# Forgetting attention into a SiLU MLP on one core: zero matmuls at the start, score tiles and MLP work in a new order, q and k turned together

## The chip, the core and the metric

The kernel runs on one core of a Trainium2 chip. The core has a matrix engine (PE, with its weight loads shown as PEld), a vector engine (DVE), an engine for exp and tanh (ACT), a general engine (POOL, GpSimd), a sync engine (SP) that issues transfers, and 16 DMA engines. The metric is the device time of one execution in microseconds (us).

## What is computed

```python
# q, k, v: (8 batches, 8 heads, 576, 64); f: (8, 8, 576); w_in: (512, 2048); w_out: (2048, 512)
cum = cumsum(log(clip(f, 1e-4, 1)), -1)
scores = q @ k.T / 8 + cum[:, :, :, None] - cum[:, :, None, :]   # causal, else -1e9
x = softmax(scores) @ v                 # heads put side by side: (4608, 512)
h = x @ w_in
out = (h * sigmoid(h)) @ w_out          # (4608, 512) float32
```

## The kernel before

**Tiling.** Two heads make a pair, four pairs a batch, so there are 32 pairs, numbered p = 0 to 31. The sequence of 576 is cut into five blocks, the last of 64 (the tail). Everything is in one hand-written order (`manual_schedule`): each engine runs its instructions in the order in which the code issues them, and waits on what it needs.

**Attention of a pair.** `scores(p, t)` (L270) makes four score tiles, t = 0 to 3, keys by queries: t0 is 512 columns for each head, t1 64 + 448, t2 320 + 192, t3 64. Two PSUM tiles are there for them (`psc`). Each matmul has 64 rows, one head; the two heads go side by side. ACT takes the exp into `uT` (L306). For the first four pairs (`first`, L273) the causal mask is added to the scores ahead of the exp (L300 on DVE, L289 on PE for t2); for all others DVE multiplies `uT` by a 0/1 mask afterwards (L320). `prep_v` (L246, POOL) scales v by the decay into `vaug`. `attend_rows` (L337) does 30 small matmuls `avr` in two groups, LO (12) and HI (18), and DVE divides into `xt` (L358, L359). `turn_pair` (L366) turns `xt` into `xT` with PE and copies on ACT for batches 0 to 3; from batch 4 on (`NTURN`) `turn_batch` (L379) does it by DMA transposes from SP, five or six pieces a batch.

**MLP.** Tokens go in 9 groups of 512. An `m1_chunk` (L391) is four matmuls of 128x512 into `hp`, tanh on ACT (L411) and a product on DVE into `gtile` (L412). An `m2_part` (L419) is four matmuls of an output block `po`; part 0 to 3 use the quarters of `w_out_bf` one after another, and after part 3 ACT copies to `osb` (four buffers) and SP stores it. Each of these units is four matmuls of 128 rows. `hp`, `po`, `avr` and the turns share four PSUM tiles (`big`).

**Order.** `work(n)` (L468) issues n MLP units, each 0.88 on a planner's clock; `spend` advances that clock and runs what `defer` has put off. `pace` (L484) decides how many units a pair gets, with `LAG` as a reserve kept for later batches. The main loop (L646) issues for each pair t0 and t1 together, a third of the units, turns and attention of the pair before, prep of v, loads; t2 and t3 together, a third; attention; and the rest. In batch 1 (pairs 4 to 7) attention's LO and HI parts stand apart.

**Loads.** q and k of batches 0 and 1, and q of batch 2 (`RAW`), come as float32, are cast on POOL (L193, L202) and turned by PE (`turn_first` L206, `transposes` L227; DVE copies them out). The others are loaded and cast by POOL's DMAs in blocks (`load_qk`, L123, tile `mp`), and turned by DMA transposes on SP (`turn_qk`, L131), one for q and one for k, into `qT` and `kT`. From batch 6 on the first blocks' turns are deferred by 9 on the planner's clock. POOL also issues w_in (L548, after the casts of the first three pairs) and w_out (L542, after vaug of pair 4).

**Start.** Batch 0 is done with no MLP work between; the first MLP unit follows its end (L632).

Of the kernel before, what the change touches and what calls it, by code (L numbers as in the profile page):

```python
# [19 lines left out]
def kernel(  # L20
# [19 lines left out]
    NB = 5  # L40
# [9 lines left out]

    const = ctx.enter_context(tc.tile_pool(name="const", bufs=1))
    ident_bf = const.tile([P, P], BF16, name="ident_bf")
    ident_f = const.tile([P, P], FP32, name="ident_f")
# [6 lines left out]
    vaugs = [const.tile([P, NB, 2, DV], BF16, name=f"vaug{i}") for i in range(NVA)]  # L60
    kTs = [const.tile([P, NPB, NB * P], BF16, name=f"kT{i}") for i in range(2)]
    us = [const.tile([P, 2, UW], BF16, name=f"uT{i}") for i in range(3)]

    xp = ctx.enter_context(tc.tile_pool(name="xp", bufs=4))
    qkp = ctx.enter_context(tc.tile_pool(name="qkp", bufs=2))
    vp = ctx.enter_context(tc.tile_pool(name="vp", bufs=2))
# [9 lines left out]
    NTURN = 4  # L76
    LAG = 10.0
    MOST = 9.0
# [5 lines left out]
    def qk_tiles(b):  # L84
        qkT[b] = (qkp.tile([P, NPB, S], BF16, name="qT", tag="qT"), kTs[b % 2])

# [36 lines left out]
    def load_qk(b, c, which):  # L123
        t = sbp.tile([P, DM], BF16, name="mp", tag="mp", bufs=16)
        raw[b, c, which] = t
        nc.gpsimd.dma_start(  # L126
            out=t[: bs[c], :].rearrange("p (h d) -> p h d", h=H),
            in_=(q, k)[which][b, :, c * P : c * P + bs[c], :].rearrange("h p d -> p h d"),
        )

    def turn_qk(b, c, which):  # L131
        if b not in qkT:
            qk_tiles(b)
        n = bs[c]
        nc.sync.dma_start_transpose(
            out=qkT[b][which][:, :, c * P : c * P + n], in_=raw[b, c, which][:n, :]
        )
# [16 lines left out]
    def decay_sum():  # L154
        lnf = f_sb
        cum = evp.tile([BH, S], FP32, name="cum", tag="ev")
        nc.vector.tensor_tensor_scan(
            out=cum[:, :], data0=lnf[:, :], data1=lnf[:, :], initial=0.0,
            op0=ALU.add, op1=ALU.bypass,
        )  # L160
        mid = const.tile([BH, 1], FP32, name="mid")
        nc.vector.tensor_scalar_mul(out=mid[:, :], in0=cum[:, S - 1 : S], scalar1=0.5)
        cumc = cum
        nc.vector.tensor_scalar(
            out=cumc[:, :], in0=cum[:, :], scalar1=mid[:, 0:1], scalar2=None,
            op0=ALU.subtract,
        )
# [38 lines left out]
    def turn_first(which):  # L206
        qk_tiles(0) if 0 not in qkT else None
        m = cast[0, 0, which].rearrange("p c h d -> p c (h d)")
        tp = big([P, SM], BF16, "tpqk")
        for c in range(NB - 1):  # L210
            nc.tensor.transpose(tp[:, c * P : (c + 1) * P], m[:, c, :], ident_bf[:, :])
        nc.vector.tensor_copy(
            out=qkT[0][which][:, 0, 0:SM].rearrange("x (p c) -> x p c", c=NB - 1),
            in_=tp[:, :].rearrange("x (c p) -> x p c", c=NB - 1),
        )

# [53 lines left out]
    def scores(p, t):  # L270
        qT, kT = (x[:, p % NPB, :] for x in qkT[p // NPB])
        u = us[p % 3]
        first = p < NPB  # L273
        sc = psc.tile([P, 2, 512], FP32, name="sc", tag="sc")
# [231 lines left out]
    def retire(p):  # L506
        b, j = divmod(p, NPB)
        if j < NPB - 1:
            return
        for c in range(NB):  # L510
            defer(2.5 + 1.2 * c, lambda c=c: turn_batch(b, c))
        for g in range(b * S // TG, (b + 1) * S // TG):
            c = ((g + 1) * TG - b * S - 1) // P
            defer(6.2 + 1.2 * c, lambda g=g: made(g + 1))
# [8 lines left out]
    for b in range(NEARLY, B):  # L523
        for i, group in enumerate([(0, 1), (2,), (3, 4)]):
            at = NPB * b - 4 + min(i, 1) if b == NEARLY else NPB * b - 7 + i
            late = 1 if b == NEARLY + 1 and len(RAW[NEARLY]) == 2 else 0
            for c in group:
                for w in range(2):
                    if w in RAW.get(b, ()):
                        continue  # L530
                    add(fetch, at + late, load_qk, b, c, w)
                    if b <= NEARLY + 1:
                        to = min(at + late + (2 if b == NEARLY else 3), NPB * b - 2)
                        add(plan, to, turn_qk, b, c, w)
                    elif i == 0 and b - 2 >= NTURN:
                        add(plan, NPB * b - 4, defer, 9.0, partial(turn_qk, b, c, w))
                    else:
                        add(plan, NPB * b - 4 + min(i, 1), turn_qk, b, c, w)
                add(plan, NPB * b - 5 + i + (b == NEARLY), load_v, b, c, nc.sync)
# [11 lines left out]

    with tc.manual_schedule():
        nc.scalar.dma_start(out=f_sb[:, :], in_=f.rearrange("b h s -> (b h) s"))
        load_main(0, 0, 2)
# [17 lines left out]
        make_identity(nc, ident_f)  # L572
        for kT in kTs:
            nc.vector.memset(kT[:, :, S:], 0.0)
        for u in us:
# [17 lines left out]
        load_w(w_in_bf, moe_w_in, DFF // 2, DFF)  # L593
        for w in range(2):
            turn_first(w)
        scores(0, 0)
        turn_first_tails()
        scores(0, 1)
        decay_sum()
        scores(0, 3)  # L600
        transposes(1, 0)
        scores(0, 2)
        decay_turn()
        prep_v(0)
# [8 lines left out]
        for p in range(1, NPB):  # L613
# [32 lines left out]
        for p in range(NPB, NP):  # L646
# [6 lines left out]
            due -= n  # L653
            n1, n2 = (n + 2) // 3, (n + 1) // 3
            n3 = n - n1 - n2
            scores(p, 0)
            scores(p, 1)
            spend(0.4)
            work(n1)
            ahead = RAW.get((p + 1) // NPB, ())  # L660
            rows = NPB < p < NPB * NEARLY
            if 0 in ahead:
                transposes(p + 1, 0)
# [71 lines left out]
```

## Time and profile before

| what | us |
|---|---|
| median of 3 runs (lowest to highest) | 359.81 (359.74 to 360.06) |
| the profiled execution | 359.25 |
| its span | 357.5 |
| PE busy, share of the span | 336.3 (94%) |
| ACT, DVE, POOL busy | 211.9, 191.7, 119.6 |
| moved by DMA | 44.92 MB |

The page gives each engine's busy share in 40 slices of the span, in tenths. Other views are answers of the trace: the timeline of an engine (start, length, engine, source line, operation, output<-inputs, rows*columns and shapes, count; in brackets idle time before it and what ended that), the waits of an engine (total, times, longest), and a source line's own instructions. PE's matmuls overlap and the end of each is modelled, so the cost of a run of matmuls is read from start to start.

### The profile page before, as it was taken

To read this page: it belongs to the slowest core of one execution; us is meant where nothing else is said; L and a number is where in the kernel's file an instruction comes from. 1 tells how busy PE (TensorE), PEld (TensorE's weight loads), DVE (VectorE), ACT (ScalarE), POOL (GpSimd) and SP (SyncE) were. 2 spreads that over 40 slices of the span, in tenths; PEclk is the share of its full clock that TensorE was granted. 3 is DMA by queue.
4 is the path that set the end of the run, shared out by engine and by line. 5 is a ranking of instruction groups with operands and counts; after the bars stand their busy time and mean duration, and the time that the engine had idled before them with its cause. 6 is when DMAs were issued, how large, how long until landed. Compare 5 with 4: busy or idle time off the path is not lost.

```text
span 357.5 us, 7026 instructions
## 1 busy us (share of the span) xinstructions
PE 336.3 (94%) x2656; PEld 168.4 (47%) x2697; DVE 191.7 (54%) x450; ACT 211.9 (59%) x345; POOL 119.6 (33%) x207
## 2 busy tenths in 40 slices
PE   2797989999999999999999999999999999999995
PEld 1455445554555445544454453444444454444442
DVE  4664895538743675348543791567237723744300
ACT  4566674558753986388647764676468615644421
POOL 5563598239554235423564250110301000000000
PEclk9999999999999999999999999999999999999999
DMA  8899999999997998399969994452240014000021
GB/s 220 213 208 315 192 193 222 155 210 170 148 150 117 163 150 78 89 170 142 124 122 152 130 166 123 100 117 75 74 83 31 1 68 118 2 29 29 31 76 71
DMA packets 142514, 44.92 MB, mean 126 GB/s; under 512 B 129616, under 2 KB 136784, under 8 KB 142480
## 3 DMA queue, kind: packets, MB, share of 16 engines
q1 hardware_dynamic: 87664, 33.64, 42.5%
q0 software_dynamic: 54736, 10.69, 38.4%
q8 instruction: 21, 0.34, 0.4%
q10 hardware_dynamic: 80, 0.15, 0.2%
q14 instruction: 13, 0.11, 0.1%
HBM read 36.85 MB, written 9.44 MB: 129 GB/s over the span
## 4 chain that ended last, share of the span: by engine, by line
PE 82%; DVE 6%; ACT 4%; DMA 3%; issue 3%; POOL 1%; SPq 0%; ACTq 0%
PE po L425 33%; PE hp L400 30%; PE avr L349 7%; PE sc L281 7%; DVE gtile L412 2%; ACT uT L306 2%; DMA xT<-xt 2%; PE tpx L371 2%; DVE uT L320 2%; PE tpqk L235 2%; ACT th L411 1%; DMA whole<-in_k_dram 1%; DVE xt L359 1%; PE sc L289 1%; DVE qT L240 1%
## 5 line engine op out<-in xcount | busy, mean ns | idle before, releaser
L400 PE MATMUL hp<-xT,w_in_bf 128*128 128x512 bf16 x556 | 135.8, 380 | 3.2 <-DVE gtile L412 0.8
L425 PE MATMUL po<-w_out_bf,gtile 128*128 128x512 bf16 x555 | 133.7, 379 | 1.4 <-DVE gtile L412 0.4
L412 DVE SCALAR_TENSOR_TENSOR gtile<-th,hp 128x512 bf16<-128x512 bf16 x144 | 96.0, 685 | 52.2 <-ACT th L411 50.3
L306 ACT ACTIVATE uT<-sc 128x1024 bf16<-128x1024 f32 (+1 forms) x128 | 101.3, 850 | 24.9 <-PE sc L281 15.9
L411 ACT ACTIVATE th<-hp 128x512 bf16<-128x512 f32 x144 | 84.8, 613 | 50.0 <-PE hp L400 46.2
L251 POOL TENSOR_TENSOR vaug<-vm,wT 128x512 bf16<-128x512 f32 x64 | 45.4, 729 | 132.7 <-PE avr L349 121.4
L400 PEld LDWEIGHTS <-w_in_bf 128*128 128x128 bf16 x576 | 53.1, 98 | 65.2 <-issue 6.1
L425 PEld LDWEIGHTS <-gtile 128*128 128x128 bf16 x576 | 53.6, 98 | 62.9 <-issue 2.4
L320 DVE TENSOR_TENSOR uT<-uT,mask 128x256 bf16<-128x256 bf16 (+1 forms) x112 | 35.3, 337 | 66.2 <-ACT uT L306 66.0
L434 ACT ACTIVATE osb<-po 128x512 f32<-128x512 f32 x36 | 21.7, 602 | 46.7 <-PE po L425 46.7
L281 PE MATMUL sc<-qT,kT 64*128 64x64 bf16 (+4 forms) x384 | 37.3, 287 | 5.5 <-ACT uT L306 2.2
L349 PEld LDWEIGHTS <-uT 128*128 128x128 bf16 x960 | 33.7, 98 | 6.4 <-issue 0.7
L349 PE MATMUL avr<-vaug,uT 128*128 128x65 bf16 x960 | 36.2, 195 | 0.2 <-POOL vaug L259 0.2
L359 DVE TENSOR_TENSOR xt<-avr,rr 128x384 bf16<-128x384 f32 x64 | 31.4, 491 | 2.3
L281 PEld LDWEIGHTS <-kT 64*128 64x128 bf16 x384 | 15.3, 95 | 30.1 <-issue 21.0
L126 POOL DMA_DIRECT2D mp<-in_k_dram x30 | 25.9, 865 | 1.0 <-DMA mp<-in_k_dram 1.0
L126 POOL DMA_DIRECT2D mp<-in_q_dram x25 | 22.2, 887 | 1.3 <-DMA w_out_bf<-in_moe_w_out_dram 0.5
L358 DVE RECIPROCAL rr<-avr 128x6 f32<-128x6 f32 x64 | 11.7, 183 | 18.6 <-PE avr L349 18.5
L377 ACT COPY xT<-tpx 128x512 bf16<-128x512 bf16 (+7 forms) x32 | 11.2, 404 | 17.0 <-PE tpx L371 16.9
L193 POOL CAST m<-whole 128x512 bf16<-128x512 f32 x20 | 11.9, 607 | 15.0 <-DMA whole<-in_q_dram 12.4
L235 PE MATMUL tpqk<-ident_bf,m 128*128 128x128 bf16 (+1 forms) x90 | 10.9, 241 | 0.3 <-DVE gtile L412 0.3
L235 PEld LDWEIGHTS <-m 128*128 128x128 bf16 (+1 forms) x90 | 7.3, 106 | 6.3 <-issue 1.6
(47 smaller groups left out, 71.8 us busy)
## 6 DMA issues: line engine op xcount, KB each, us to landing
out_dram<-osb SPq DMA_DIRECT2D x36, 256.0 KB, 2.2
vm<-in_v_dram SPq DMA_DIRECT2D x32, 256.0 KB, 4.7
mp<-in_k_dram POOLq DMA_DIRECT2D x24, 128.0 KB, 6.2
whole<-in_q_dram SPq DMA_DIRECT2D x5, 512.0 KB, 9.7
mp<-in_q_dram POOLq DMA_DIRECT2D x20, 128.0 KB, 4.8
w_in_bf<-in_moe_w_in_dram POOLq DMA_DIRECT2D x2, 1024.0 KB, 11.2
w_out_bf<-in_moe_w_out_dram POOLq DMA_DIRECT2D x4, 512.0 KB, 10.7
whole<-in_k_dram SPq DMA_DIRECT2D x3, 512.0 KB, 9.5
```

Source lines behind the costliest of these rows:

```text
L126: nc.gpsimd.dma_start(out=t[: bs[c], :].rearrange("p (h d) -> p h d", h=H), in_=(q, k)[which][b, :, c * P : c * P + bs[c], :].rearrange("h ...
L235: nc.tensor.transpose(tp[:, c * P : c * P + n], m[:n, c, :, :].rearrange("p h d -> p (h d)"), ident_bf[:n, :n],)
L251: nc.gpsimd.tensor_tensor(out=va[:n, c0:c1, :, 0:D], in0=vm[:n, c0:c1, 2 * j : 2 * j + 2, :], in1=wT[:n, c0:c1, 2 * j + b * H : 2 * j + 2 ...
L281: nc.tensor.matmul(sc[:, i, col : col + n], lhsT=kT[r, kb * P : (kb + 1) * P], rhs=qT[r, q0 : q0 + n], start=True, stop=not pe_adds,)
L306: nc.scalar.activation(out=u[:, :, o : o + col], in_=sc[:, :, 0:col], func=ACT.Exp, scale=scale)
L320: nc.vector.tensor_tensor(out=d, in0=d, in1=mk, op=ALU.mult)
L349: nc.tensor.matmul(av[:, qb - lo, i, :], lhsT=u[:, i, o : o + P], rhs=va[:, kb, i, :], start=(kb == 0), stop=(kb == qb),)
L359: nc.vector.tensor_tensor(out=xt[:, lo:hi, 2 * j : 2 * j + 2, :], in0=av[:, :, :, 0:D], in1=r[:, 0:n, :, None].to_broadcast([P, n, 2, D]), ...
L400: nc.tensor.matmul(hp[:, :], lhsT=w_in_bf[:, cc, fc * P : (fc + 1) * P], rhs=xg[g][:, cc, :], start=(cc == 0), stop=(cc == NCC - 1),)
L411: nc.scalar.activation(out=th[:, :], in_=hp[:, :], func=ACT.Tanh, scale=0.5)
L412: nc.vector.scalar_tensor_tensor(out=gte[:, fc, :], in0=th[:, :], scalar=1.0, in1=hp[:, :], op0=ALU.add, op1=ALU.mult,)
L425: nc.tensor.matmul(po[:, :], lhsT=gte[:, fc, tb * P : (tb + 1) * P], rhs=w_out_bf[:, fc, :], start=(fc == 0), stop=(fc == NFC - 1),)
```

## The change

- PE gets matmuls of zeros (`spin`), 34 of 128x512 at the start: seven ahead of the first turn, the others among the turns, score tiles and attention of pairs 0 and 1. Their input `idle` is set to zero first on DVE.
- `turn_first` copies k in two pieces, the first 128 keys ahead.
- Score masks of pairs 4 and 5 are added ahead of the exp (t0, t1, t3).
- q and k share one tile `qkTs` for each parity of the batch. `load_qk` puts both into one tile of twice the width (8 buffers for 16), and one DMA transpose turns both (k alone in batch 2).
- `turn_batch` is issued at once at the end of a batch from 4 on, and the first q/k turns of batches 6 and 7 are no longer deferred.
- `LAG` is 14 for 10.
- In the main loop units are given out by shares of n: in batches 1 and 2 between all four score tiles, from batch 3 on 0.35 after t1, 0.1 and 0.25 after t3, and the rest.

```diff
-    kTs = [const.tile([P, NPB, NB * P], BF16, name=f"kT{i}") for i in range(2)]
+    qkTs = [const.tile([P, 2, NPB, NB * P], BF16, name=f"qkT{i}") for i in range(2)]
...
-    LAG = 10.0
+    LAG = 14.0
...
     def load_qk(b, c, which):
-        t = sbp.tile([P, DM], BF16, name="mp", tag="mp", bufs=16)
-        raw[b, c, which] = t
+        if (b, c) not in raw:
+            raw[b, c] = sbp.tile([P, 2 * DM], BF16, name="mp", tag="mp", bufs=8)
...
-    def turn_qk(b, c, which):
+    def turn_qk(b, c):
...
+        w = [x for x in range(2) if x not in RAW.get(b, ())]
         nc.sync.dma_start_transpose(
-            out=qkT[b][which][:, :, c * P : c * P + n], in_=raw[b, c, which][:n, :]
+            out=qkTs[b % 2][:, w[0] :, :, c * P : c * P + n].rearrange(
+                "x w j n -> x (w j) n"
+            ),
+            in_=raw[b, c][:n, w[0] * DM :],
         )
...
+    def spin(n):
+        ps = big([P, SM], FP32, "spin")
+        for _ in range(n):
+            nc.tensor.matmul(
+                ps[:, :], lhsT=idle[:, 0:P], rhs=idle[:, :], start=True, stop=True
+            )
...
+        for p0, p1 in ((0, P),) if which == 0 else ((0, P // 4), (P // 4, P)):
+            nc.vector.tensor_copy(
...
-        first = p < NPB
+        first = p < NPB + 2 and (t != 2 or p < NPB)
...
         for c in range(NB):
-            defer(2.5 + 1.2 * c, lambda c=c: turn_batch(b, c))
+            turn_batch(b, c)
...
-                    elif i == 0 and b - 2 >= NTURN:
-                        add(plan, NPB * b - 4, defer, 9.0, partial(turn_qk, b, c, w))
-                    else:
-                        add(plan, NPB * b - 4 + min(i, 1), turn_qk, b, c, w)
+                else:
+                    to = NPB * b - 4 + min(i, 1)
+                add(plan, to, turn_qk, b, c)
...
+        nc.vector.memset(idle[:, :], 0.0)
...
-        for w in range(2):
-            turn_first(w)
+        spin(7)
+        turn_first(0)
+        spin(4)
+        turn_first(1)
+        spin(2)
         scores(0, 0)
...
+            def step(share):
+                nonlocal left, part
+                part += share * n
+                k = min(left, int(part + 0.5))
+                part -= k
+                left -= k
+                work(k)
+
             scores(p, 0)
+            spend(0.3)
+            step(0.2 if b <= NEARLY else 0.0)
             scores(p, 1)
-            spend(0.4)
-            work(n1)
+            spend(0.3)
+            step(0.2 if b <= NEARLY else 0.35)
...
-            if early:
-                work(n2 // 2)
+            step(0.1 if b <= NEARLY else 0.0)
             scores(p, 2)
+            spend(0.3)
+            step(0.2 if b <= NEARLY else 0.0)
             scores(p, 3)
-            spend(0.3)
+            spend(0.2)
             if 1 in ahead:
                 transposes(p + 1, 1)
+            step(0.1)
             if rows:
                 attend_rows(p - 1, HI)
-            work(n2 - n2 // 2 if early else n2)
+            step(0.0 if b <= NEARLY else 0.25)
             if b >= NEARLY and j > 0:
                 attend_rows(p - 1)
                 spend(1.2)
-            work(n3)
+            work(left)
```

More of the change, by code (lines that the diff above doesn't have):

```diff
@@ L51 @@
     const = ctx.enter_context(tc.tile_pool(name="const", bufs=1))
+    idle = const.tile([P, SM], BF16, name="idle")
     ident_bf = const.tile([P, P], BF16, name="ident_bf")
@@ L60 @@
     vaugs = [const.tile([P, NB, 2, DV], BF16, name=f"vaug{i}") for i in range(NVA)]
-    kTs = [const.tile([P, NPB, NB * P], BF16, name=f"kT{i}") for i in range(2)]
+    qkTs = [const.tile([P, 2, NPB, NB * P], BF16, name=f"qkT{i}") for i in range(2)]
     us = [const.tile([P, 2, UW], BF16, name=f"uT{i}") for i in range(3)]
     xp = ctx.enter_context(tc.tile_pool(name="xp", bufs=4))
-    qkp = ctx.enter_context(tc.tile_pool(name="qkp", bufs=2))
     vp = ctx.enter_context(tc.tile_pool(name="vp", bufs=2))
@@ L84, in qk_tiles @@
     def qk_tiles(b):
-        qkT[b] = (qkp.tile([P, NPB, S], BF16, name="qT", tag="qT"), kTs[b % 2])
+        qkT[b] = (qkTs[b % 2][:, 0], qkTs[b % 2][:, 1])
     def raw_tile():
@@ L123, in load_qk @@
     def load_qk(b, c, which):
-        t = sbp.tile([P, DM], BF16, name="mp", tag="mp", bufs=16)
-        raw[b, c, which] = t
+        if (b, c) not in raw:
+            raw[b, c] = sbp.tile([P, 2 * DM], BF16, name="mp", tag="mp", bufs=8)
         nc.gpsimd.dma_start(
-            out=t[: bs[c], :].rearrange("p (h d) -> p h d", h=H),
+            out=raw[b, c][: bs[c], which * DM : (which + 1) * DM].rearrange(
+                "p (h d) -> p h d", h=H
+            ),
             in_=(q, k)[which][b, :, c * P : c * P + bs[c], :].rearrange("h p d -> p h d"),
         )
-    def turn_qk(b, c, which):
+    def turn_qk(b, c):
         if b not in qkT:
@@ L134, in turn_qk @@
         n = bs[c]
+        w = [x for x in range(2) if x not in RAW.get(b, ())]
         nc.sync.dma_start_transpose(
-            out=qkT[b][which][:, :, c * P : c * P + n], in_=raw[b, c, which][:n, :]
+            out=qkTs[b % 2][:, w[0] :, :, c * P : c * P + n].rearrange(
+                "x w j n -> x (w j) n"
+            ),
+            in_=raw[b, c][:n, w[0] * DM :],
         )
@@ L211, in turn_first @@
             nc.tensor.transpose(tp[:, c * P : (c + 1) * P], m[:, c, :], ident_bf[:, :])
[L212 to L215, printed above, removed]
+        dst = qkT[0][which][:, 0, 0:SM].rearrange("x (p c) -> x p c", c=NB - 1)
+        for p0, p1 in ((0, P),) if which == 0 else ((0, P // 4), (P // 4, P)):
+            nc.vector.tensor_copy(
+                out=dst[:, p0:p1, :],
+                in_=tp[:, :].rearrange("x (c p) -> x p c", c=NB - 1)[:, p0:p1, :],
+            )
     def turn_first_tails():
@@ L528 @@
                 for w in range(2):
[L529 to L534, printed above, removed]
-                    elif i == 0 and b - 2 >= NTURN:
-                        add(plan, NPB * b - 4, defer, 9.0, partial(turn_qk, b, c, w))
-                    else:
-                        add(plan, NPB * b - 4 + min(i, 1), turn_qk, b, c, w)
+                    if w not in RAW.get(b, ()):
+                        add(fetch, at + late, load_qk, b, c, w)
+                if b <= NEARLY + 1:
+                    to = min(at + late + (2 if b == NEARLY else 3), NPB * b - 2)
+                else:
+                    to = NPB * b - 4 + min(i, 1)
+                add(plan, to, turn_qk, b, c)
                 add(plan, NPB * b - 5 + i + (b == NEARLY), load_v, b, c, nc.sync)
@@ L572 @@
         make_identity(nc, ident_f)
-        for kT in kTs:
-            nc.vector.memset(kT[:, :, S:], 0.0)
+        for t in qkTs:
+            nc.vector.memset(t[:, 1, :, S:], 0.0)
         for u in us:
@@ L593 @@
         load_w(w_in_bf, moe_w_in, DFF // 2, DFF)
-        for w in range(2):
-            turn_first(w)
+        spin(7)
[3 more added lines that the diff above has]
+        spin(2)
         scores(0, 0)
         turn_first_tails()
+        spin(2)
         scores(0, 1)
+        spin(3)
         decay_sum()
         scores(0, 3)
+        spin(1)
         transposes(1, 0)
+        spin(2)
         scores(0, 2)
+        spin(1)
         decay_turn()
@@ L605 @@
         transposes(1, 1)
+        spin(4)
         scores(1, 0)
+        spin(2)
         cast_both(3)
@@ L618 @@
                 transposes(p + 1, 0)
+            if p == 1:
+                spin(2)
             scores(p, 3)
@@ L623 @@
                 turn_pair(p - 2)
+            else:
+                spin(4)
             attend_rows(p - 1, LO)
@@ L653 @@
             due -= n
[L654 to L657, printed above, removed]
-            spend(0.4)
-            work(n1)
             ahead = RAW.get((p + 1) // NPB, ())
             rows = NPB < p < NPB * NEARLY
+            left, part = n, 0.0
+            def step(share):
[5 more added lines that the diff above has]
+                work(k)
+            scores(p, 0)
+            spend(0.3)
+            step(0.2 if b <= NEARLY else 0.0)
+            scores(p, 1)
+            spend(0.3)
+            step(0.2 if b <= NEARLY else 0.35)
             if 0 in ahead:
```

## The prediction

> **What bounds the kernel now.** The profiled execution took 359.25 us; its span is 357.5, so 1.75 us lie around the span. The median of the runs shown, 359.81, is 0.56 above this execution. All terms below are made against the execution and 0.56 is added at the end. I read first the page: the span by slices.
>
> ```profile
> span 357.5 us, 7026 instructions
> ...
> PE   2797989999999999999999999999999999999995
> ...
> PEclk9999999999999999999999999999999999999999
> DMA  8899999999997998399969994452240014000021
> ```
>
> A slice is 8.9 us. PE has room in the first four slices and at the end (the last store); from then on it is full. The DMA engines are full through slice 11, about 100 us. So there are two resources that can set the time: data until about 57 us (shown below), then PE. Second, PE's timeline at the start.
>
> ```profile
> 17.74 0.82 PE L349 MATMUL avr<-vaug,uT 128*128 128x65 bf16 x12 [0.17 <-POOL vaug L259]
> ...
> 19.79 0.61 PE L281 MATMUL sc<-qT,kT 64*128 64x512 bf16 x2
> ...
> 24.05 0.54 PE L349 MATMUL avr<-vaug,uT 128*128 128x65 bf16 x12
> ...
> 25.38 0.39 PE L281 MATMUL sc<-qT,kT 64*128 64x512 bf16 x2
> ...
> 34.12 4.69 PE L400 MATMUL hp<-xT,w_in_bf 128*128 128x512 bf16 x21 [0.67 <-ACT xT L377]
> ```
>
> The clock row reads 9 from the first slice, yet the same work takes 0.82 and 0.61 before about 23.4 us and 0.54 and 0.39 after it: PE runs cold for 23 us, whatever that row says. At 17.74 it waits for POOL's first vaug. MLP work runs without pause from 34.12. Third, PE's timeline around 50 us, and the loads of w_out (its source line).
>
> ```profile
> 50.16 0.61 PE L281 MATMUL sc<-qT,kT 64*128 64x512 bf16 x6 [1.02 <-DVE kT L240]
> ...
> 53.79 1.02 PE L425 MATMUL po<-w_out_bf,gtile 128*128 128x512 bf16 x3 [0.37 <-DVE gtile L412]
> ...
> 56.12 2.76 PE L425 MATMUL po<-w_out_bf,gtile 128*128 128x512 bf16 x12
> ...
> 58.71 0.52 PE L371 MATMUL tpx<-ident_bf,xt 128*128 128x128 bf16 x5
> ```
> ```profile
> L542 POOL DMA_DIRECT2D w_out_bf<-in_moe_w_out_dram x4: 747/765/803, 41.3 to 43.6; - x4
> ...
> DMA to landing us min/median/max: 8.1/10.7/13.5
> ```
>
> The four quarters of w_out are issued at 41.3 to 43.6 and land 8.1 to 13.5 later, the last at 43.6 + 13.5 = 57.1. The 12 po matmuls at 56.12 are parts 1 to 3 of the first output block; part 3, the last four, needs the last quarter and starts at 56.12 + 8 x 0.216 = 57.85. It had 0.8 us to spare. Fourth, PE's waits from 58 us to the end, which are few.
>
> ```profile
> PE hp L400 <- DVE gtile L412: 0.8, 2, 0.4
> PE tpx L371 <- DVE xt L359: 0.5, 2, 0.3
> PE sc L281 <- ACT uT L306: 0.5, 1, 0.5
> PE hp L400 <- DMA xT<-xt: 0.3, 1, 0.3
> ```
>
> Fifth, PE's timeline in batch 2, for the price of going between MLP and score matmuls.
>
> ```profile
> 104.55 2.76 PE L425 MATMUL po<-w_out_bf,gtile 128*128 128x512 bf16 x12
> 107.25 0.42 PE L281 MATMUL sc<-qT,kT 64*128 64x320 bf16 x6
> 107.60 1.90 PE L425 MATMUL po<-w_out_bf,gtile 128*128 128x512 bf16 x8
> 109.34 1.07 PE L349 MATMUL avr<-vaug,uT 128*128 128x65 bf16 x30
> ```
>
> Eight MLP matmuls ahead of avr (128 rows both) take 109.34 - 107.60 = 1.74, or 0.217 each. Twelve ahead of scores take 2.70, and 12 x 0.217 is 2.60: 0.10 is lost on entering. The six score matmuls, two heads side by side, pass 320 + 192 + 64 = 576 columns, at 0.217 per 512 columns 0.24; they take 0.35: 0.11 on leaving.
>
> **Part 1: zeros' matmuls and the quarter copy of k.** 34 matmuls of 128x512 and one memset are added. The memset of idle (two of half its bytes, L574, take 0.31 together) stands first on DVE, which later waits 2.44 us for f: nothing. k's first copy in two pieces costs DVE one start more (a copy of 64 columns takes 0.18) and frees the first score tile by up to half of 0.69, all of it before 17.7: nothing. A warm 128x512 costs 0.217; cold is not shown, and twice that, 0.43, is my estimate (avr x18 takes 1.17 cold, 0.72 warm; less about 0.2 of last drain each, 1.9 times). Seven run before the first cast is there at 4.5; the other 27 must fit what PE idles between 4.5 and 17.74: 27 x 0.217 = 5.9 us warm, against 4.3 idle in PE's timeline and about 4 that the remaining 9 of cold work give back. Attending cannot begin before POOL's vaug at 17.70, which hangs on POOL's queue (casts that wait for loads, the two w_in issues, then vaug) and does not move. From there the cold rows to 23.4 shorten: avr 0.82 and 1.10 by a third, each score tile by 0.2 to 0.4; with exps of 1.02 each on ACT in between, the first MLP run comes 1.7 earlier by my count (0 if the spins overrun, 2.5 if all cold rows shrink freely).
>
> **Part 2: what takes that gain back.** Score masks of pairs 4 and 5 move ahead of the exp (0.43 each on PSUM, L300, for 0.29 to 1.69 of the mask products at 43.9 to 48.8), and score tiles are set apart; that may remove the 1.02, 0.37 and 0.27 waits near 50. So PE could be at part 3 up to 3.6 us earlier, at about 54.3. But w_out's last quarter lands at 57.1: POOL issues it after vaug of pair 4, which waits 4.49 us for v's load (POOL's timeline at 39.85), behind loads that keep the engines full since 16 us, and the change moves none of these. So 0.75 is all that reaches pair 6 (bounds: 0 and 3.6).
>
> **Part 3: score tiles set apart in batches 1 and 2.** In the two PE orders, scores are entered from MLP 40 times before and 60 after, left for MLP 51 and 69; also 5 more turns of q or k, whose last matmul has 64 rows, are followed by MLP instead of scores. Pair by pair: 4 switches more in pairs 4 to 7 and 11, 6 more in 8, 9, 10. Pairs 4 and 5 lie under the wait for w_out: free there (8 x 0.1 = 0.8 if that cover went). Pairs 6 to 11: 4 + 4 + 6 + 6 + 6 + 4 = 30, times 0.095 = **+2.85** on a full PE (bounds 30 x 0.06 and 30 x 0.11: 1.8 to 3.3).
>
> Waits that go: one gtile wait of 0.44 in batch 2 (the other, 0.33 at 128, follows attend_rows as before), with the 0.16 that a modelled end hides: -0.6 (0 to -0.8). The xt waits stay, their order is the same. A new one: in pair 9 the turn of x follows attend_rows after one unit (0.87) where two stood; DVE must first finish a gtile (0.69), then two reciprocals and products (0.20 + 0.56 + 0.18 + 0.42), about 2 us less the 0.9 of avr: +0.4 (0 to 0.9).
>
> The Trainium skill speaks to the price of part 3 ("TensorE: Matmul & The Clock Gate", Part 2, step 1): PE pulls a weight load ahead of running matmuls where row groups do not conflict or a background buffer takes it. By that reading a switch is free and the 2.85 falls away; the trace agrees for 128 rows after 128 rows (0.217 each) and not at the switch (0.10 in, 0.11 out).
>
> **Part 4: turns, x at once, reserve.** One transfer turns q and k: 55 become 30. SP's issue is 1.2 each and may double for twice the data, which bounds it at no change in all. In before the last transfer of batch 3 is issued at 96 and takes some 5 to land, scores of pair 12 start at 115.4; later batches have more. It now waits on SP for both loads, which POOL issues side by side; v loads and out stores stand behind it, none of them due. Nothing. The x turns are no longer deferred by 2.5 and more planner units: SP now stands at them until xt is made, then issues five or six at 1.25 and two q/k turns, some 13 us in which out stores wait; PE ends two or three output blocks in that time and osb has four buffers: nothing. In return the xT wait goes: -0.3 - 0.16 = -0.45 (0 to -0.6). The reserve moves units of the later batches; the place where only one unit stood between two score groups (wait 0.5 for uT) is filled: -0.5 (0 to -0.5). Elsewhere 8 MLP matmuls stand between two groups where 12 stood; PE work is the same.
>
> **Sum.** -0.75 + 2.85 - 0.6 + 0.4 - 0.45 - 0.5 = +0.95. 359.25 + 0.95 = 360.2; with 0.56, **360.8 us**. Slower by 0.27%; about 0.2% (0.7 us) is what a measurement here can tell from no change.
>
> **Rivals.**
> - *The switches cost nothing when set apart*: PE loads a score tile's weights during the MLP matmul before it, as it does between MLP matmuls: 360.8 - 2.85 = 357.9, faster. Against it: every switch in batch 2 shows the 0.1. It decides from a price under 0.03. Chance 0.08.
> - *w_out does not hold PE* because its last quarter lands early with the rest: up to 2.85 more arrives, 357.9, faster. Against: DMA full from the first slice. Chance 0.10.
> - *The waits weigh more than I took*: all 2.1 of the fourth view go where I counted 1.24, and no new one comes: 360.8 - 0.86 - 0.4 = 359.5, same. For it: two exps of 1.02 back to back hold up tanh and so hp's release, and they are now apart. Against: the xt waits keep their order. Chance 0.27.
> - *The zeros do not warm PE* (the change does not do what it says): 27 x 0.43 = 11.6 against 4.3 idle, 7.3 late at 17.7; with 1.7 of the waits near 50 gone part 3 is 5.6 late, not 0.75 early: 367. It decides from about half the spins cold. Against: durations fell at 23.4 after some 4 us with hardly a pause. Chance 0.05.
> - The forecast: 0.50.
>
> Faster 0.20 (the first two and 0.02 of the third), same 0.28 (the rest of the third, 0.03 of the forecast), slower 0.52. The range takes in both faster rivals and, above, a forecast in which none of the 1.55 of waits goes: 357.8 to 362.4.
>
> **What would show it.** Right: score tiles of 64x512 at 0.39 before 10 us; avr first at 17.7; MLP without pause near 32.4; a PE wait for w_out's DMA between 51 and 57 us; the turn of x at 58.7 now near 58; pair 12 some 1.9 us later than before; fewer waits of hp for gtile. Wrong: no wait for w_out, or 12 MLP matmuls ahead of a score tile in 2.60.

## The result: slower by 1.4%, and the profile after

Changed: 365.46 us, median of six runs (362.94 to 366.09). Before: 359.77, median of six. The ratio is **1.0139, with a 95% interval of 1.0101 to 1.0178**. The prediction, 360.8 with a range of 357.8 to 362.4, had the direction; the size lies outside its range. The execution that was profiled is the slowest of the six.

The profiled execution of the changed kernel took 366.09, span 363.9. These lines of its page answer to those shown of before:

```profile
span 363.9 us, 7051 instructions
...
PE   8898969999999999999999999999999999999995
...
PEclk9999978999999999999999999999999999999999
DMA  8899899999959987879879996590320022000011
```

One slice is 9.1 us. The new thing is in the clock row (PEclk, the clock that was granted to PE, in tenths of full speed): the sixth and seventh slice (45 to 64 us) read 7 and 8. The first digits are 9 as in before, though PE begins cold again, as the timeline shows. PE's timeline at the start of the changed kernel:

```profile
1.20 3.17 PE L179 MATMUL spin<-idle 128*128 128x512 bf16 x7 [1.20 <-DVE idle L565]
...
7.05 0.39 PE L296 MATMUL sc<-qkT 64*128 64x512 bf16 x2
...
18.19 0.52 PE L364 MATMUL avr<-vaug,uT 128*128 128x65 bf16 x12 [0.43 <-POOL vaug L274]
...
32.75 4.69 PE L415 MATMUL hp<-xT,w_in_bf 128*128 128x512 bf16 x21 [0.68 <-ACT xT L392]
```

Seven zeros' matmuls take 3.17, so cold ones are about 0.43 each. The first score tile already takes 0.39, where before it took 0.61 until 23 us. The first MLP run begins at 32.75 for 34.12: 1.37 us are won, and then lost with more. PE's timeline of the changed kernel in pairs 4 and 5:

```profile
46.38 0.20 PE L296 MATMUL sc<-qkT 64*128 64x64 bf16 x2 [0.21 <-ACT uT L321]
47.59 0.52 PE L250 MATMUL tpqk<-ident_bf,m 128*128 128x128 bf16 x5 [1.01 <-DVE gtile L427]
48.29 1.04 PE L415 MATMUL hp<-xT,w_in_bf 128*128 128x512 bf16 x4 [0.19 <-DVE qkT L259]
51.14 0.61 PE L296 MATMUL sc<-qkT 64*128 64x512 bf16 x2 [1.81 <-DVE qkT L255]
51.68 1.89 PE L415 MATMUL hp<-xT,w_in_bf 128*128 128x512 bf16 x4
...
54.44 1.49 PE L415 MATMUL hp<-xT,w_in_bf 128*128 128x512 bf16 x3 [0.33 <-issue]
...
57.08 1.03 PE L440 MATMUL po<-w_out_bf,gtile 128*128 128x512 bf16 x4
```

Two idle times, 1.01 and 1.81, each ended by DVE. Then four MLP matmuls take 1.89 instead of 1.04: the granted clock in the trace is half from 50.21 to 57.04. PE gets to part 0 of the first output block at 57.08, when all of w_out has landed (56.94), so the wait for w_out that the prediction named does not appear at all. Its absence was the prediction's own first sign of being wrong.

Where the difference lies, by the start of the first score tile of a pair in the two profiled executions:

| stretch | before | changed | difference | predicted |
|---|---|---|---|---|
| start to pair 4 | 42.26 | 40.89 | -1.37 | -1.7 |
| pair 4 to pair 6 | 16.78 | 21.64 | +4.86 | +0.95 (of the 1.7, only 0.75 gets through) |
| pair 6 to pair 12 | 56.36 | 59.46 | +3.10 | +2.65 (2.85 - 0.6 + 0.4) |
| pair 12 to the end of the span | 242.07 | 241.88 | -0.19 | -0.95 (-0.45 - 0.5) |
| around the span | 1.78 | 2.22 | +0.44 | 0 |
| sum | 359.25 | 366.09 | +6.84 | +0.95 |

So 3.9 of the 5.9 us by which the sum was missed lie in two pairs.

### The profile page after: what moved, and what is told of

Same layout as the page of the kernel before. It is cut to its first block, busy times and chain, and to the rows that moved or that the text cites. A ratio compares the mean times of both kernels' runs of the same rounds, so it can differ in the third digit from the quotient of the medians.

```text
span 363.9 us, 7051 instructions
## 1 busy us (share of the span) xinstructions
PE 347.4 (95%) x2687; PEld 168.7 (46%) x2731; DVE 192.0 (53%) x452; ACT 211.5 (58%) x345; POOL 120.2 (33%) x207
## 4 chain that ended last, share of the span: by engine, by line
PE 86%; ACT 4%; DVE 3%; DMA 2%; issue 2%; SPq 1%; POOL 1%; ACTq 0%; DVEq 0%
PE po L440 34%; PE hp L415 33%; PE avr L364 7%; PE sc L296 7%; ACT uT L321 3%; PE tpqk L250 2%; PE tpx L386 2%; DMA whole<-in_k_dram 1%; ACT th L426 1%; DVE xt L374 1%; DVE gtile L427 1%; DMA vm<-in_v_dram 1%; PE spin L179 1%; DVE qkT L255 1%; PE sc L304 0%
## 5 line engine op out<-in xcount | busy, mean ns | idle before, releaser
L415 PE MATMUL hp<-xT,w_in_bf 128*128 128x512 bf16 x556 | 139.0, 383 | 2.8 <-ACT xT L392 0.7
L440 PE MATMUL po<-w_out_bf,gtile 128*128 128x512 bf16 x553 | 135.5, 379 | 1.2 <-issue 0.2
L321 ACT ACTIVATE uT<-sc 128x1024 bf16<-128x1024 f32 (+1 forms) x128 | 102.9, 853 | 36.9 <-PE sc L296 21.9
L426 ACT ACTIVATE th<-hp 128x512 bf16<-128x512 f32 x144 | 85.1, 615 | 48.7 <-PE hp L415 42.3
L415 PEld LDWEIGHTS <-w_in_bf 128*128 128x128 bf16 x576 | 52.2, 98 | 63.5 <-issue 7.9
L440 PEld LDWEIGHTS <-gtile 128*128 128x128 bf16 x576 | 52.7, 98 | 61.3 <-issue 3.2
L335 DVE TENSOR_TENSOR uT<-uT,mask 128x512 bf16<-128x512 bf16 (+1 forms) x106 | 32.9, 328 | 71.5 <-ACT uT L321 70.8
L296 PE MATMUL sc<-qkT 64*128 64x64 bf16 (+4 forms) x384 | 38.9, 281 | 3.3 <-DVE qkT L255 1.8
L296 PEld LDWEIGHTS <-qkT 64*128 64x128 bf16 x384 | 15.0, 94 | 36.9 <-issue 27.7
L255 DVE COPY qkT<-tpqk 128x512 bf16<-128x512 bf16 x18 | 12.3, 683 | 1.7 <-PE tpqk L250 1.6
L179 PE MATMUL spin<-idle 128*128 128x512 bf16 x33 | 11.2, 449 | 1.2 <-DVE idle L565 1.2
```

Source lines behind the costliest of these rows:

```text
L296: nc.tensor.matmul(sc[:, i, col : col + n], lhsT=kT[r, kb * P : (kb + 1) * P], rhs=qT[r, q0 : q0 + n], start=True, stop=not pe_adds,)
L321: nc.scalar.activation(out=u[:, :, o : o + col], in_=sc[:, :, 0:col], func=ACT.Exp, scale=scale)
L335: nc.vector.tensor_tensor(out=d, in0=d, in1=mk, op=ALU.mult)
L415: nc.tensor.matmul(hp[:, :], lhsT=w_in_bf[:, cc, fc * P : (fc + 1) * P], rhs=xg[g][:, cc, :], start=(cc == 0), stop=(cc == NCC - 1),)
L426: nc.scalar.activation(out=th[:, :], in_=hp[:, :], func=ACT.Tanh, scale=0.5)
L440: nc.tensor.matmul(po[:, :], lhsT=gte[:, fc, tb * P : (tb + 1) * P], rhs=w_out_bf[:, fc, :], start=(fc == 0), stop=(fc == NFC - 1),)
```

## The experiments

**Theory: a ring.** In pairs 4 and 5 the mask's add stands on DVE ahead of the exp. With one MLP unit (tanh on ACT, product on DVE) between two score tiles, DVE's add is followed by ACT's exp, behind it in ACT's queue the unit's tanh, then DVE's product for that unit, and behind that product in DVE's queue the next add. Nothing in this ring overlaps. DVE's timeline and then ACT's, changed kernel:

```profile
42.23 0.43 DVE L315 TENSOR_TENSOR sc<-sc,maskadd 128x256 f32<-128x256 f32 x1
44.23 0.69 DVE L427 SCALAR_TENSOR_TENSOR gtile<-th,hp 128x512 bf16<-128x512 bf16 x1 [1.58 <-ACT th L426]
44.84 0.42 DVE L315 TENSOR_TENSOR sc<-sc,maskadd 128x256 f32<-128x256 f32 x1
46.84 0.69 DVE L427 SCALAR_TENSOR_TENSOR gtile<-th,hp 128x512 bf16<-128x512 bf16 x1 [1.58 <-ACT th L426]
47.45 0.68 DVE L255 COPY qkT<-tpqk 128x512 bf16<-128x512 bf16 x1
```
```profile
42.69 1.02 ACT L321 ACTIVATE uT<-sc 128x1024 bf16<-128x1024 f32 x1 [1.10 <-DVE sc L315]
43.61 0.59 ACT L426 ACTIVATE th<-hp 128x512 bf16<-128x512 f32 x1
45.30 1.03 ACT L321 ACTIVATE uT<-sc 128x1024 bf16<-128x1024 f32 x1 [1.09 <-DVE sc L315]
46.22 1.08 ACT L426 ACTIVATE th<-hp 128x512 bf16<-128x512 f32 x2
```

Read across: add 42.23, exp 42.69, tanh 43.61, product 44.23, next add 44.84. One turn takes 2.61, in which DVE idles 1.58 and ACT 1.1, for a score tile and a unit that PE does in 1.3. The copies of the next q and k (47.45 and later) stand behind all this on DVE, and PE waits for them.

**Rivals.** The split itself, with score tiles one by one, breaks up the queues, masks or no masks. Or the stall is small and the half clock is the loss. Or the mask's place ahead of the exp costs, whoever adds it.

All runs in one table; stretches are from each one's profiled execution, ratios from timed runs against before on the same chip (before: 359.77 to 360.15 there).

| run | to pair 4 | 4 to 6 | 6 to 12 | 12 to end | median | ratio (95%) |
|---|---|---|---|---|---|---|
| before | 42.26 | 16.78 | 56.36 | 242.07 | | |
| changed | 40.89 | 21.64 | 59.46 | 241.88 | 365.46 | 1.0139 (1.0101 to 1.0178) |
| e1 masks late | 40.47 | 17.03 | 59.44 | 241.82 | 361.38 | 1.0033 (1.0013 to 1.0053) |
| e2 batch 1 together | 40.78 | 18.32 | 58.61 | 241.83 | 362.47 | 1.0061 (1.0041 to 1.0082) |
| e3 zeros alone | 40.71 | 17.76 | 55.85 | 243.05 | 359.07 | 0.9967 (0.9944 to 0.9990) |
| e4 split alone | 44.05 | 17.35 | 59.64 | 241.86 | 363.72 | 1.0101 (1.0062 to 1.0140) |
| e5 both undone | 41.13 | 17.95 | 56.55 | 241.84 | 359.01 | 0.9953 (0.9929 to 0.9977) |
| e6 masks alone | 43.85 | 19.97 | 55.76 | 241.85 | 362.29 | 1.0053 (1.0031 to 1.0076) |
| e7 turns alone | 42.36 | 17.10 | 56.39 | 240.86 | 359.08 | 0.9966 (0.9945 to 0.9987) |
| e8 clock kept | 40.30 | 20.00 | 59.46 | 241.82 | 363.68 | 1.0092 (1.0063 to 1.0120) |
| e9 best | 40.37 | 17.69 | 56.21 | 240.86 | 357.56 | 0.9925 (0.9898 to 0.9953) |
| e10 v later | 40.66 | 16.84 | 62.54 | 240.85 | 362.94 | 1.0077 (1.0051 to 1.0103) |
| e11 masks on PE | 40.68 | 17.07 | 59.45 | 241.85 | 361.24 | 1.0036 (1.0018 to 1.0055) |
| e12 shares alone | 43.99 | 16.71 | 56.36 | 244.19 | 362.36 | 1.0060 (1.0038 to 1.0083) |

### e1: the changed kernel, masks of pairs 4 and 5 after the exp again

```diff
-        first = p < NPB + 2 and (t != 2 or p < NPB)
+        first = p < NPB
```

> The changed kernel with one part undone: pairs 4 and 5 get their masks after the exp again. Loop theory (the adds ahead of the exp put DVE and ACT in a ring: add 0.43, exp 1.02, tanh 0.60, product 0.69, about 2.6 us for each score tile with its unit, where PE needs 1.2): pair 6 begins near 58 instead of 62.5, the clock is not cut near 50, and the whole is about 361 (4 below the changed kernel). Split theory (score tiles set apart by MLP units starve PE whichever way the mask is applied): pair 6 still begins after 61 and the whole stays above 364.

Measured: pair 6 starts at 57.50 instead of 62.53, the clock stays whole, and the time falls from ratio 1.0139 to 1.0033. DVE's timeline of e1, same units, same score tiles:

```profile
42.11 0.29 DVE L335 TENSOR_TENSOR uT<-uT,mask 128x256 bf16<-128x256 bf16 x1 [0.22 <-ACT uT L321]
42.60 0.69 DVE L427 SCALAR_TENSOR_TENSOR gtile<-th,hp 128x512 bf16<-128x512 bf16 x1 [0.20 <-ACT th L426]
43.52 0.55 DVE L335 TENSOR_TENSOR uT<-uT,mask 128x256 bf16<-128x256 bf16 x1 [0.23 <-ACT uT L321]
44.01 0.69 DVE L427 SCALAR_TENSOR_TENSOR gtile<-th,hp 128x512 bf16<-128x512 bf16 x1
```

Masks come 1.41 apart (42.11, 43.52) where the adds came 2.61 apart: behind the exp the mask is in nobody's way on ACT. And PE's timeline of e1 now has the wait that was predicted, because PE is early enough to meet it:

```profile
56.31 1.02 PE L440 MATMUL po<-w_out_bf,gtile 128*128 128x512 bf16 x3 [0.38 <-DMA w_out_bf<-in_moe_w_out_dram]
```

The split alone does not make the stall: the rival falls. What is left of the loss, +3.08 in pairs 6 to 11, was put down to the split there; e4 and e5 test it.

### e2: the changed kernel, batch 1's score tiles two by two, masks early

```diff
-            step(0.2 if b <= NEARLY else 0.35)
+            step(0.2 if b <= NEARLY else 0.35, n1)
...
+                if tog:
+                    left -= k
+                    work(k)
+                    return
```
Here `tog` holds for batch 1, and k is the number of units that the kernel before gave at that place.

> The changed kernel with batch 1's score tiles issued two by two again, as before; batch 2's stay apart and the masks of pairs 4 and 5 stay ahead of the exp. Loop theory: two adds, two exps and then the units' tanhs pass DVE and ACT in groups, the ring is turned half as often; pair 6 begins near 60, whole about 362 to 363. Split theory: pair 6 begins near 58, no cut of the clock, whole 361 less 1.5 for switches that are no longer made in batch 1's pairs 6 and 7: about 360.

Measured: pairs 4 to 6 take 18.32, between e1 and the changed kernel. The early masks still cost: PE's waits of e2 from 34 to 62 us are

```profile
PE po L440 <- DVE gtile L427: 1.8, 1, 1.8
PE tpqk L250 <- DVE gtile L427: 0.9, 1, 0.9
PE sc L296 <- DVE qkT L255: 0.5, 1, 0.5
```

3.2 us of waits for DVE, against 0.9 in e1. So it is the early mask, and the one-by-one order makes it worse. Not all of these waits are the mask's: without it e4 waits 1.7 for DVE's copies, and e5, which has batch 1 as here, 1.8 in all. The stretch of e5 is only 0.38 shorter than e2's, since w_out, late there (57.85, here 56.62), holds it by 0.8.

### e3: the kernel before, with the zeros' matmuls alone

```diff
+        spin(7)
+        turn_first(0)
+        spin(4)
+        turn_first(1)
+        spin(2)
...
```

> The kernel before with the zeros' matmuls alone. If w_out's landing near 57 holds PE as the prediction said: pair 4 begins 1.4 earlier, pair 6 at most 0.8 earlier, the whole about 359.0. If it does not hold: pair 6 and the end come 1.4 earlier, about 358.4. If zeros' matmuls have a cost later (power, PSUM slots): no gain.

Measured: pair 4 is 1.55 earlier, pair 6 only 0.57 earlier. The rest stands in one line of PE's timeline of e3:

```profile
57.28 1.02 PE L433 MATMUL po<-w_out_bf,gtile 128*128 128x512 bf16 x4 [1.34 <-DMA w_out_bf<-in_moe_w_out_dram]
```

The prediction's first two steps hold: the zeros bring 1.4 to 1.55, and w_out lets 0.6 of it through (0.75 was said). How much passes differs from one execution to the next: over the 14 profiled ones the last quarter of w_out landed between 55.76 and 57.85. This profiled execution also lost 0.81 at pair 24 to a late transfer of q, which is most of why its last stretch is 0.98 longer.

### e4: the kernel before, with batches 1 and 2 split alone

```diff
             scores(p, 0)
+            spend(0.3 if b <= NEARLY else 0.0)
+            step(0.2)
             scores(p, 1)
...
+            step(0.1)
             scores(p, 2)
+            spend(0.3 if b <= NEARLY else 0.0)
+            step(0.2)
```

> The kernel before with score tiles set apart in batches 1 and 2 alone (masks after the exp, turns, reserve and start as before). The prediction's price: 30 switches of 0.095 in pairs 6 to 11, +2.85, plus 0.8 in pairs 4 and 5 unless waits there cover it, less 0.6 of gtile waits, plus 0.7 for the turn of x in pair 9: 362.5 to 363.5. Split theory of the stall: pair 6 begins 3 or more later than before and the whole is 365 or more. Loop theory: pair 6 within 1 us of before.

Measured: pairs 4 to 6 +0.57, pairs 6 to 12 +3.28, nothing after. Its start is 1.8 late in the profile: without zeros' matmuls the clock rose at 28.1 us here and at 23.8 in before. The split begins only with pair 4, so that part is not the split's. The split's own price is thus 3.3 in batches 1 and 2 behind pair 6, the largest term of the prediction with its size nearly right.

### e5: the changed kernel, masks late and batches 1 and 2 two by two

The edits of e1 and e2 together, with `tog` for both batches.

> The changed kernel with masks of pairs 4 and 5 after the exp and score tiles of batches 1 and 2 together, both as before; zeros, turns, x at once, reserve and the later batches' shares stay. If the switches are what is left after the masks are put back (pairs 6 to 12 took 3.1 longer with them): pair 6 near 58.3, held by w_out at 57, pairs 6 to 12 in 56.4 and the whole 361.4 - 3.1 + 0.8 = about 359. If something in the turns or the shares costs as well: 360 or more.

Measured: 0.9953, faster than before, and pairs 6 to 12 within 0.2 of before. PE waits 0.8 for w_out. Between e1 and e5 lies the split alone, in batches 1 and 2: 1.0033 - 0.9953 is 0.8%, 2.9 us.

### e6: the kernel before, with the early masks alone

```diff
-        first = p < NPB
+        first = p < NPB + 2 and (t != 2 or p < NPB)
```

> The kernel before with the mask adds of pairs 4 and 5 ahead of the exp alone. Ring theory with tiles two by two: DVE and ACT pass the ring once for two tiles, so some 2 us of waits of PE for DVE come on (1.8 and 0.9 were seen in e2), less the 0.8 that w_out holds back anyway: pair 6 begins 1 to 2 later, whole 361 to 362. If the masks hurt only between tiles set apart: no change, 360.

Measured: pairs 4 to 6 +3.19, median ratio 1.0053. PE waits for DVE again, and the profiled execution has its clock halved from 58.57 to 61.99. PE's timeline of e6:

```profile
57.03 1.02 PE L425 MATMUL po<-w_out_bf,gtile 128*128 128x512 bf16 x4 [1.78 <-DVE gtile L412]
...
58.87 1.17 PE L349 MATMUL avr<-vaug,uT 128*128 128x65 bf16 x18
59.85 3.81 PE L425 MATMUL po<-w_out_bf,gtile 128*128 128x512 bf16 x12
```

avr x18 takes 1.17, the cold value, and twelve MLP matmuls 3.81 for 2.76. One line of the diff does this in the old order too. Alone it costs about 1.9 us by the medians (0.53%); in the changed order, changed to e1, 1.06% or 3.8 us.

### e7: the kernel before, with the turns, x at once and the reserve alone

```diff
-    LAG = 10.0
+    LAG = 14.0
...
-            defer(2.5 + 1.2 * c, lambda c=c: turn_batch(b, c))
+            turn_batch(b, c)
...
+            out=qkTs[b % 2][:, w[0] :, :, c * P : c * P + n].rearrange(
+                "x w j n -> x (w j) n"
+            ),
```
It has no zeros' matmuls; its masks come after the exp and its units go by thirds. k's first copy in two pieces and the planner's smaller steps are in it.

> The kernel before with one transfer for q and k, x turned at once, reserve 14, the planner's clock steps of the changed kernel and k's first copy in two pieces; no zeros, masks after the exp, units by thirds. Prediction's term: -0.95 (a wait of 0.5 for uT and 0.45 for xT go). From the changed kernel's traces, where pair 12 to the end took 0.2 less than before: -0.2. A cost of the wider turns would show as a wait of scores for a DMA.

Measured: pair 12 to the end -1.21, against -0.95 predicted for this group. Of PE's waits there (0.5 for uT, 0.3 for xT, 0.3 for gtile before) only the last is left. The time around the span is 2.21 instead of 1.78: so it is in every kernel with these edits (2.21 to 2.24) and in none without (1.77 to 1.80). No run takes these edits apart, so which of them adds the 0.44 is not known.

### e8: the changed kernel, with zeros' matmuls in the idle times of pairs 4 and 5

```diff
+        for _ in range({(4, 3): 3, (5, 0): 8, (5, 1): 3}.get((p, t), 0)):
+            nc.tensor.matmul(
+                sc[:, 0, :], lhsT=idle[:, 0:P], rhs=idle[:, :], start=True, stop=True
+            )
```

> The changed kernel with 14 more zeros' matmuls written into the score tiles of pair 4's t3 and pair 5's t0 and t1 just before their scores, so that PE has something to do where it waited for DVE (1.0 and 1.8). If the half clock between 50 and 57 is a cost of its own: the clock's row stays at full there, pair 6 begins about 2.5 earlier than in the changed kernel (near 60) and the whole is about 363. If the stall of DVE and ACT alone makes the time: 365 or more, with the clock at full.

Measured: the clock stays whole and pair 6 starts at 60.30, 2.2 earlier than in the changed kernel. Of that, 0.59 was there at pair 4 already, ahead of the edit; pairs 4 to 6 take 20.00 for 21.64, 1.64 less. By the ratios it is 1.0139 - 1.0092, 0.47%, 1.7 us, though the two intervals overlap. The ring is still there: e1 takes 17.03, 2.97 less. The 14 zeros take 14 x 0.217 = 3.0 of PE's time themselves, so 2.97 is an upper bound of the ring's part, and 1.64 a lower bound of what half speed added to it. PE's waits of e8 from 34 to 62 us begin with

```profile
PE sc L300 <- DVE qkT L255: 0.4, 1, 0.4
PE tpqk L250 <- DVE gtile L431: 0.3, 1, 0.3
```

where the changed kernel has 1.8 and 1.0.

### e9: the changed kernel without the masks and without any new shares

Masks late, units by thirds in all batches; zeros, turns, x at once and the reserve stay.

> The changed kernel with masks of pairs 4 and 5 after the exp and units by thirds in all batches: the zeros, the wider turns, x at once and the reserve remain. If gains add: e3's 0.6 to 1.1 and e7's 1.0 below before, so 358.2 to 358.5, with pair 6 held near 58.4 by w_out; e5 had 359.0, so the later batches' shares would be worth 0.6 or so. If the shares cost nothing: 359.0 again.

Measured: **357.56 us, ratio 0.9925 (0.9898 to 0.9953), faster than both kernels.** PE's waits of e9 from 34 to 62 us:

```profile
PE sc L296 <- DVE qkT L255: 1.1, 1, 1.1
PE po L440 <- DMA w_out_bf<-in_moe_w_out_dram: 0.7, 1, 0.7
PE po L440 <- DVE gtile L427: 0.7, 1, 0.7
```

Against e5 it differs in the shares of the later batches: 12 to end 240.86 for 241.84, 1.0 us, 0.75 of it between pairs 12 and 15. PE's timeline in pair 14 shows one such place, in e5:

```profile
131.49 1.90 PE L415 MATMUL hp<-xT,w_in_bf 128*128 128x512 bf16 x8
133.32 0.39 PE L296 MATMUL sc<-qkT 64*128 64x320 bf16 x4
133.89 0.20 PE L296 MATMUL sc<-qkT 64*128 64x64 bf16 x2 [0.18 <-ACT uT L321]
```

and in e9:

```profile
129.91 2.76 PE L415 MATMUL hp<-xT,w_in_bf 128*128 128x512 bf16 x12
132.61 0.42 PE L296 MATMUL sc<-qkT 64*128 64x320 bf16 x6
```

Twelve MLP matmuls ahead of t2 and t3 cover the exps of t0 and t1 here; eight do not, and t3 comes apart from t2. On ACT the copies of xT stand ahead of these exps (in e5 from 131.30, the exps from 131.87); in pair 13, where no such copies do, eight are enough. From pair 14's first score tile to pair 15's e5 takes 8.84 and e9 8.31. The seven kernels with the new shares take 8.83 to 8.84 there, the seven without 8.30 to 8.31.

### e10: e9, with v of batch 2 loaded two pairs later

```diff
-                add(plan, NPB * b - 5 + i + (b == NEARLY), load_v, b, c, nc.sync)
+                at_v = NPB * b - 5 + i if b > NEARLY else NPB * b - 2 + (i > 1)
+                add(plan, at_v, load_v, b, c, nc.sync)
```

> As e9, and v of batch 2 is loaded two pairs later, so that w_out's four loads no longer stand behind its first three blocks (3.7 us of the DMA engines). If w_out's landing is what holds PE at 57: w_out lands 2 to 3 earlier, PE's wait for it goes, pair 6 begins 0.8 to 1.3 earlier, whole 0.8 to 1.3 below e9. If not: same as e9. Loss, if v then comes late for pair 8: a wait of avr for vaug after 85.

A miss. w_out landed 0.75 earlier than in e9, its wait went, and pair 6 came 0.56 earlier; but the profiled executions differ by up to 2.1 in that landing, so one pair of them does not show that the edit did it. PE then waited for a cast that stood behind `prep_v`, which waited for the late v, in POOL's queue. PE's timeline of e10:

```profile
83.46 0.77 PE L250 MATMUL tpqk<-ident_bf,m 128*128 128x128 bf16 x5 [4.09 <-POOL m L206]
84.01 0.70 PE L296 MATMUL sc<-qkT 64*128 64x320 bf16 x6
84.64 6.70 PE L415 MATMUL hp<-xT,w_in_bf 128*128 128x512 bf16 x20
```

4.09 of waiting, and the clock half from 82.32 to 89.15. POOL had stood 17.37 for v until 81.32, and the cast came at 82.81, behind that `vaug`.

### e11: the changed kernel, early masks added by PE instead of DVE

```diff
-        pe_adds = adds if first and t == 2 else []
+        pe_adds = adds if first and (t == 2 or p >= NPB) else []
```

> The changed kernel with the masks of pairs 4 and 5 still ahead of the exp, but added by PE (two 128-wide matmuls of the mask for each tile, as t2 of batch 0 has) and not by DVE. Ring theory: DVE has no add between two products, the ring is cut, pair 6 near 57.5 to 58, clock at full, whole near e1's 361.4. If it is the mask's place ahead of the exp, on whichever engine, that delays: 364 or more.

Measured: pairs 4 to 6 take 17.07, like e1, and the ratio is 1.0036. The mask is still ahead of the exp; only DVE is out of the ring. Its products on DVE stand 1.40 to 1.46 apart (41.41, 42.87, 44.27). That decides the last rival: the ring is DVE's add behind DVE's product, not the mask's place.

### e12: the kernel before, with the shares of the later batches alone

```diff
+            step(0.35, n1)
...
+            step(0.1)
...
+            step(0.25, n2 - n2 // 2 if early else n2)
```
The new shares hold from batch 3 on; batches 1 and 2 keep the old counts.

> The kernel before with the later batches' (3 to 7) shares of units and planner steps alone: 0.35 after t1, 0.1 and 0.25 after t3, the rest at the end. The prediction gave it no cost. From e5 (241.8 from pair 12 to the end) against e7 (240.9): +1.0, about 361. If that difference belongs to the zeros or to chance: 360.

Measured: 12 to end +2.12. PE's waits of e12 from 62 us to the end begin with

```profile
PE sc L281 <- ACT uT L306: 1.6, 3, 0.9
```

for 0.5 in before. Where fewer or no MLP matmuls are left between the two groups of score tiles, PE stands at t2 or t3 before an exp has freed the tile. PE's timeline of e12 in pair 21 shows a place with none; before has four there, and one wait of 0.52:

```profile
191.81 0.61 PE L281 MATMUL sc<-qT,kT 64*128 64x512 bf16 x6
193.32 0.40 PE L281 MATMUL sc<-qT,kT 64*128 64x320 bf16 x4 [0.90 <-ACT uT L306]
194.24 0.20 PE L281 MATMUL sc<-qT,kT 64*128 64x64 bf16 x2 [0.52 <-ACT uT L306]
```

With the larger reserve the shares cost 1.0 (e5 to e9), alone 2.1. By the starts of the pairs 0.86 of the 2.1 lies in pair 21 and 0.53 in pair 14, as in e5; 0.62 in pair 28 stays unexplained. Its pair 4 is 1.7 late in the profile, by a clock that rose only at 28 us.

## Why the prediction was right in direction and wrong in size

**The bound and the start: right.** Warm score tiles by 7 us, the first MLP run 1.4 earlier (1.7 said), and w_out passing on 0.57 of 1.55 in e3 (0.75 said). The first vaug, which lets attending begin and was said not to move, ended at 18.14 instead of 17.69; in the nine profiled executions with zeros it ended between 17.55 and 18.39, so this lies within their spread. From the first avr matmul to the first MLP matmul it is 12.48 for 14.30 in before: 1.8 won, close to the 1.7. e1, e3, e5, e9 and e11 show the wait for w_out's last quarter where it was said to be, with 0.4, 1.3, 0.8, 0.7 and 0.2.

**Part 2, the step that failed.** "... that may remove the 1.02, 0.37 and 0.27 waits near 50. ... So 0.75 is all that reaches pair 6 (bounds: 0 and 3.6)." The move of the mask was bounded as a gain only. In its place PE was at pair 6 3.49 later: 4.24 us of miss, more than all the rest. The working compared 0.43 of add with 0.29 to 1.69 of product, that is, busy time on DVE, which was not the bound. It did not ask what stands behind the waiting add in DVE's queue and behind the waiting exp in ACT's. The four durations were in the profile of before: add 0.43, exp 1.02, tanh 0.60, product 0.69, in sum 2.74; the turn took 2.61. "Pairs 4 and 5 lie under the wait for w_out: free there" was right for the switches (e1 still meets the wait at 56.31), but a cover of about 2 us (0.8 to spare, 1.4 won at the start) was not enough for this.

**The clock: not in the sum at all.** At least 1.6 of the 4.24 are half speed after the stall (e8). In the changed kernel's six runs, the four with a mean clock of 0.991 took 365.44 to 366.09; the two with 0.995 and 1.000 took 362.94 and 363.26, near e8's 363.68.

**Part 3: right.** +3.10 for a predicted +2.65 in pairs 6 to 11; e4 has +3.28 and e1 +3.08. The wait of x in pair 9 came, larger than 0.4: PE's timeline of the changed kernel has it in two pieces.

```profile
100.19 0.34 PE L386 MATMUL tpx<-ident_bf,xt 128*128 128x128 bf16 x3 [0.33 <-DVE xt L374]
100.74 0.36 PE L386 MATMUL tpx<-ident_bf,xt 128*128 128x128 bf16 x2 [0.21 <-DVE xt L374]
```

Those are 0.54 by the profile, and 0.7 with the modelled ends. The rival that a switch is free falls: the 30 switches cost 0.10 each, by 3.10 with the 0.6 that went added back and the 0.7 that came taken off, and with the split undone (e5) the stretch is back within 0.2 of before. The Trainium skill ("TensorE: Matmul & The Clock Gate", Part 2, step 1) has weight loads pulled ahead of running matmuls where row groups do not conflict or the load goes to the background weight buffer; the switches here do not come out free. The prediction's second sign of being wrong, 12 MLP matmuls ahead of a score tile in 2.60, did not come: e9 has 2.70 (129.91 to 132.61).

**Part 4: right for the edits it weighed, wrong for those it did not.** Turns, x and reserve bring -1.21 (e7) for -0.95. Two terms were taken as nothing: the later shares, +1.0 (e5 against e9), where "8 MLP matmuls stand between two groups where 12 stood; PE work is the same" overlooked that eight do not cover two exps where copies of xT stand ahead of them on ACT (0.53 in pair 14, 0.22 in pair 12); and 0.44 around the span (e7).

**The direction** does not hang on the step that failed: with the masks late (e1) the kernel is still slower than before, by 0.33%, through the split. That this is near the 0.27% of the sum is in part chance: the two terms taken as nothing add 1.4, and pair 6 comes 0.8 earlier than was counted (57.50, before 59.04).

**The rivals.** w_out did hold PE in the five kernels named above. The waits of the fourth view went mostly as counted. The zeros warmed PE. The rival at 367 was near in time for a cause that did not occur; no rival had the queues of DVE and ACT, though a mask moved ahead of the exp is exactly an added wait, and it should have been one.

**What stays open.** Which edit of e7 adds the 0.44 around the span. How the loss of pairs 4 and 5 divides between ring and half speed beyond the two bounds of e8. Why the clock of kernels without zeros rises at 23.8 in some profiled executions (before, e7) and near 28 in others (e4, e6, e12): no run here tells the two apart.

## What to carry to other kernels

When an operation moves to the other side of an exp, do not compare its busy times: follow the queues of both engines once round, and add the durations of all that must happen in a row; if the sum per tile (here 2.6 us) is above what the bounding engine needs for it (1.3), it is the new bound. A stall of the matrix engine can have a second price at half clock (here where PE's waits came to 1.8 us or more within 3.4 us), so give predicted PE waits of that size a term for it too. And test edits of one change apart: here zeros, turns, x and reserve gain 0.75%, and the masks, the split and the shares together lose more than that.

## What the runs showed of the hardware

**The clock changed in steps of 3.413 us, and it fell behind steps in which PE idled about half the time or more.** Every stretch of one clock between two changes in these traces is a whole number of steps (44.37 = 13, 6.83 = 2, 3.41 = 1, 307.20 = 90). PE's idle time, as the profile gives it, was counted in the steps of each of the 14 profiled executions after the first rise, the steps behind the last matmul included. Behind every full-speed step with 2.10 us idle or more the clock fell at once, as in e10 (2.95, the step to 82.32); behind every step with 1.59 or less it stayed. Between these both occur: it fell at 1.86 (changed, the step to 50.21) and 1.78 (e6, to 58.57), and it stayed at 1.89 (e10) and 1.82 (e12), both in the step with the last matmul. So idle time alone gives the border only to within 1.59 and 2.10. e2 waits 1.8 in one piece and keeps its clock; the end of a step falls within the wait and leaves 1.30 idle in the first. That the changed kernel's runs differ in clock fits this, but only one was profiled. The rise does not follow the same count: e12 has three steps without any idle time before it rises at 28.06, before has one and rises at 23.77. The Trainium skill ("TensorE: Matmul & The Clock Gate", Part 1) gives a free-running window of about 3.4 us, and these traces agree; it has the clock fall after an idle window, and here a step with about half of it idle was enough, so the measurement decides.

**Zeros open the clock.** Matmuls of zeros, with a few turns among them, raise it at 3.9 to 7.2 us; without them it rises at 23.8 or about 28. The start then varies less: the first score tile of pair 4 lies at 40.3 to 41.1 in the nine profiled executions with zeros, and at 42.3 to 44.1 in the five without.

**The clock row of the page does not show the cold start.** It reads 9 in the first slices of before, where score tiles take 0.61 for 0.39; the first recorded clock there is the rise at 23.8.
